# Rounding w_out by column groups in order of use, with seven products in all batches, nine attention slots beside it, and sums over keys in four column tiles

## Chip, cores and metric

One core of one Trainium2 chip. The metric is device time in microseconds (us) of that core, the median of several executions. The kernel before takes 1590.8 us (1589.6 to 1591.5).

## The reference, cut to what matters

```python
# q, k, v: (8, 12, 448, 64) float32; w_in (768, 2048) and w_out (2048, 768): float64
q_n, k_n = rmsnorm(q, g_q), rmsnorm(k, g_k)
scores = scale * q_n @ k_n.T                 # per batch and head
attn = exp(scores - max); attn = attn / (attn.sum(-1) + 1e-9)
x = (attn @ v) -> (3584, 768)                # heads side by side
h = x @ w_in;  g = h - tanh(h)
out = g @ w_out                              # (3584, 768)
```

The weights are float64 and are read as pairs of 32-bit words. The kernel rounds them to float32 itself, with instructions of ScalarE, VectorE and GpSimd.

## The kernel before: the parts that matter

The MLP uses a scheme of seven products in place of eight: seven combinations of weight blocks are made once, put into DRAM, and each batch streams them back through a ring of tiles (`w_f`). Attention goes by *slots*: one slot is two heads of one batch. Between the pieces of a slot, `run(gap)` puts MLP products into TensorE's order of instructions, so that other engines have time for their part.

```python
EARLY = 20                    # pieces of 384 weights per partition rounded in the opening
ring = pool("ring", bufs=6)   # w_f tiles
xp = pool("xp", bufs=9)

def scores(s, half): ...      # 4 score products in 4 "sc" banks, then exponentials on ScalarE
def add(s): ...               # VectorE adds the four key blocks, from the third slot beside the MLP on

def totals(s, dn):            # sum over keys: ones (64 columns), two column tiles
    for i, p in enumerate(parts):
        for h in range(2):
            nc.tensor.matmul(dn[h * D : (h + 1) * D, :S], lhsT=ones[:CP, :D], rhs=p[:, h, :], ...)
    rd = sp.tile([P, S], F32, name="rd")
    nc.vector.reciprocal(rd, dn[:, :S])

def slot(s):
    scores(s + 1, 0)
    load(s + 2, "v")
    run(gap)
    norm(s + 3)
    rd = totals(s, sc_bank())
    divide(s, values(s, sc_bank()), rd)
    run(gap)
    scores(s + 1, 1); add(s + 1)
    run(gap)
    turn(s + 2, sc_bank(), sc_bank()); norm_q(s + 3); load(s + 4, "kq")
    run(gap)

# [cut] project_first: batch 0 takes a plain product with w_out (96 products of 448 columns),
# w_out stays in SBUF while it is rounded; its combinations are made in the second half of it.
```

Six slots stand in the opening, where no weights are ready; three slots stand beside the first part of the MLP and three beside the plain product.

Of the kernel before, what the change touches and what calls it, by code (L numbers as in the profile page):

```python
# [67 lines left out]
def round_weight_a(nc, raw, dst):  # L68

    lo, hi = raw[:, :, 0], raw[:, :, 1]  # L70
    nc.scalar.activation(dst, hi.bitcast(F32), AF.Abs, scale=2.0**-16)
    nc.scalar.mul(lo, lo.bitcast(U32), 2.0**-29)


def round_weight_b(nc, raw, dst):

    bits = dst.bitcast(I32)
    nc.vector.tensor_scalar(out=dst, in0=dst, scalar1=HI_MIN, scalar2=HI_MAX, op0=ALU.max, op1=ALU.min)
    nc.vector.tensor_scalar(  # L79
        out=bits, in0=bits, scalar1=4, scalar2=1, op0=ALU.logical_shift_left, op1=ALU.logical_shift_right  # L80
    )
    nc.vector.scalar_tensor_tensor(  # L82
        out=bits, in0=raw[:, :, 1], scalar=-(2**31), in1=bits, op0=ALU.bitwise_and, op1=ALU.bitwise_or
    )


def round_weight_c(nc, raw, dst):

    bits = dst.bitcast(I32)
    nc.gpsimd.tensor_tensor(out=bits, in0=bits, in1=raw[:, :, 0], op=ALU.add)  # L90


def bounded_path(tc, ctx, q, k, v, moe_w_in, moe_w_out, out, g_col, ident, ones, neg_half):
# [26 lines left out]
    EARLY = 20  # L120
# [4 lines left out]
    STEPS = 7 * (SETS + HC)  # L125
# [6 lines left out]
    ring = pool("ring", bufs=6)  # L132
# [7 lines left out]
    xp = pool("xp", bufs=9)  # L140
    gp = pool("gp", bufs=1)
    wp_stack = ctx.enter_context(ExitStack())
# [9 lines left out]
    def load(s, names):  # L152
# [17 lines left out]
    w_out_sb = [wp.tile([P, DM], F32, name=f"w_out{f}") for f in range(CF)]  # L170
    w_in_dram = {
        (j, p): scratch.tile([P, 2 * HALF], F32, name=f"w_in{j}_{p}") for j in range(SETS) for p in range(1, 8)
    }
    BLOCKS = {1: 0, 2: 1, 4: 2, 7: 3, 5: 4, 6: 5, 3: 6}
    w_out_dram = scratch.tile([P, 7, HC, HF, P], F32, name="w_out")
    w_in_words, w_out_words = weight_words(moe_w_in), weight_words(moe_w_out)
    raws = {}
    stage = gp.tile([P, CF, S], F32, name="gT").bitcast(I32).rearrange("p f s -> p (f s)")
    NSTAGE = CF * S // DM

    def built(j, p):

        return w_out_sb[HF * (j % 2) + p].rearrange("p (f n) -> p f n", f=2)

    def weight_piece(n):

        if n < 2 * CF:
            j, f, blk = n // 8, n % 8 // 4, n % 4
            p, low, i = ((1, 0, 0), (0, 1, 0), (4, 1, 1), (2, 0, 1))[blk]
            return 2 * j + f + low * HF, i, built(j, p)[:, f]  # L190
        i, f = (n - 2 * CF) // CF, n % CF
        if i == 1:
            f = f // 2 + f % 2 * HF
        return f, i, w_out_sb[f][:, i * HALF : (i + 1) * HALF]

    def weight_load(n):

        f, i, _ = weight_piece(n)
        if n < EARLY:
            raw = stage[:, n % NSTAGE * DM : (n % NSTAGE + 1) * DM].rearrange("p (f w) -> p f w", w=2)  # L200
        else:
            raw = wp.tile([P, HALF, 2], I32, name="w_raw", bufs=4)
        if n < 2 * CF:
            rows = w_in_words[i * HALF : (i + 1) * HALF, f * 2 * P : (f + 1) * 2 * P]
            nc.sync.dma_start(
                out=raw.rearrange("p (c f) w -> p c (f w)", c=HC),
                in_=rows.rearrange("(c p) f -> p c f", p=P),
            )
        else:
            nc.sync.dma_start(  # L210
                out=raw.rearrange("p f w -> p (f w)"),
                in_=w_out_words[f * P : (f + 1) * P, 2 * i * HALF : 2 * (i + 1) * HALF],
            )
        raws[n] = raw
# [4 lines left out]
    def place_free(n):  # L219

        if n < EARLY:
            return n - NSTAGE < done[2]
        return n - 4 < max(done[2], EARLY)

    def weight(to):

        while done[1] < min(to, 4 * CF):
            n = done[1]
            round_weight_a(nc, raws[n], weight_piece(n)[2])
            if n:  # L230
                round_weight_b(nc, raws[n - 1], weight_piece(n - 1)[2])
            done[1] = n + 1
            finish_weights(n - 1 if n < EARLY else n)
            while done[0] < min(n + 6, 4 * CF) and place_free(done[0]):
                weight_load(done[0])
                done[0] += 1
            if kept[1] < kept[0] and n >= 8 * kept[0] + 3:
                keep_weights()
        if done[1] == 4 * CF > done[2]:
            round_weight_b(nc, raws[4 * CF - 1], weight_piece(4 * CF - 1)[2])  # L240
            finish_weights(4 * CF)

    def finish_weights(to):
        while done[2] < to:
            round_weight_c(nc, raws.pop(done[2]), weight_piece(done[2])[2])
            done[2] += 1
            if done[2] % 8 == 0 and done[2] <= 2 * CF:
                combine_weights(done[2] // 8 - 1)

    def combine_weights(j):  # L250
        a = [built(j, p) for p in range(8)]
        nc.vector.tensor_tensor(out=a[5], in0=a[0], in1=a[4], op=ALU.add)
        nc.gpsimd.tensor_tensor(out=a[7], in0=a[1], in1=a[0], op=ALU.subtract)
        nc.vector.tensor_tensor(out=a[6], in0=a[5], in1=a[1], op=ALU.subtract)
        nc.vector.tensor_tensor(out=a[3], in0=a[2], in1=a[6], op=ALU.subtract)
        kept[0] = j + 1

    def keep_weights():
        j = kept[1]
        for p in ORDER:  # L260
            nc.sync.dma_start(out=w_in_dram[j, p], in_=built(j, p).rearrange("p f n -> p (f n)"))
        kept[1] = j + 1

    def combine_w_out(f):

        a11, a21 = (w_out_sb[f][:, i * HALF : (i + 1) * HALF] for i in range(2))
        a12, a22 = (w_out_sb[f + HF][:, i * HALF : (i + 1) * HALF] for i in range(2))
        t = [ring.tile([P, 8 * P], F32, name="w_f") for _ in range(2)]
        s3, s1, s2, s4 = (t[i // 2][:, i % 2 * HALF : (i % 2 + 1) * HALF] for i in range(4))
        nc.vector.tensor_tensor(out=s1, in0=a21, in1=a22, op=ALU.add)  # L270
        nc.gpsimd.tensor_tensor(out=s3, in0=a11, in1=a21, op=ALU.subtract)
        nc.vector.tensor_tensor(out=s2, in0=s1, in1=a11, op=ALU.subtract)
        nc.vector.tensor_tensor(out=s4, in0=a12, in1=s2, op=ALU.subtract)
        for n, count, src in ((0, 1, a11), (1, 2, w_out_sb[f + HF]), (3, 2, t[0]), (5, 2, t[1])):
            nc.sync.dma_start(
                out=w_out_dram[:, n : n + count, :, f, :].rearrange("p k c d -> p (k c) d"),
                in_=src[:, : count * HALF].rearrange("p (k d) -> p k d", d=P),
            )
# [4 lines left out]
        for layer, count in ((0, SETS), (1, HC if b else 0))  # L283
# [5 lines left out]
    def ring_load(key, ahead):  # L289

        for n in range(len(ring_tiles), min(ring_steps.index(key) + ahead, len(ring_steps))):
            b, layer, j, p = ring_steps[n]
            t = ring_tiles[ring_steps[n]] = ring.tile([P, 8 * P], F32, name="w_f")
            if layer == 0:
                assert kept[1] > j
                nc.sync.dma_start(out=t[:, : 2 * HALF], in_=w_in_dram[j, p])
            else:
                nc.sync.dma_start(out=t, in_=w_out_dram[:, BLOCKS[p], j].rearrange("p f d -> p (f d)"))


    normed, turned, probs, sums, xT, tt = {}, {}, {}, {}, {}, {}

    def norm(s):

        rr = normed[s] = small.tile([CP, 2, 2 * NCH], F32, name="rr", bufs=3)
        for names in ("q", "k") if s == 0 else ("kq",):
            for name in names:
                rows = loaded[name, s].rearrange("p a b d -> p (a b) d")
                sq = nat.tile([CP, 2 * NCH, D], F32, name="sq", bufs=1)
                nc.gpsimd.tensor_tensor(out=sq, in0=rows, in1=rows, op=ALU.mult)  # L310
# [32 lines left out]

    def sc_bank():
# [694 lines left out]
```

## Time and profile before

| stage of the kernel before | from, to (us) | what limits it |
|---|---|---|
| opening: six slots, first weights | 0 to 117 | VectorE with rounding, by its busy time (the runs do not bear it out, see the end) |
| w_in products of batch 0 | 117 to 264 | nothing is full; TensorE waits for weights that go through DRAM |
| plain product, batch 0 | 264 to 366 | TensorE |
| seven batches, 36 slots | 366 to 1589 | TensorE, granted clock 1.00 |

### The profile page before, as it was taken

What the parts mean: (1) busy time and instruction counts of PE and PEld (TensorE: products, weight loads), DVE (VectorE), ACT (ScalarE), POOL (GpSimd) and SP (SyncE); (2) the same over time, 40 slices, a digit from 0 to 9 for tenths busy, and PEclk for the clock granted to TensorE, in tenths of its full rate; (3) what the DMA queues carried; (4) which work ended last, traced back from release to release, by engine and by line L of the source; (5) the groups of instructions that cost most, each with busy time, mean ns of one, the idle gap of its engine ahead of it and who ended that gap; (6) DMA issues with size and microseconds to landing.
All of it is one profiled execution on the core that took longest, in us unless ns stands there. A gap on an engine that the chain in (4) does not pass through costs nothing.

```text
span 1588.6 us, 19983 instructions
## 1 busy us (share of the span) xinstructions
PE 1494.3 (94%) x7440; PEld 1164.7 (73%) x7440; DVE 788.6 (50%) x1004; ACT 446.4 (28%) x870; POOL 624.4 (39%) x516
## 2 busy tenths in 40 slices
PE   3988768998999999999999999999999999999997
PEld 1336456446878878878877887787877887789997
DVE  6788558865454345434544445434544344522211
ACT  4554234512322223222331232321331232210210
POOL 6655446552452234422453235423444234311410
PEclk9999879999999999999999999999999999999999
DMA  7554575577545554555554564465454664455564
GB/s 193 177 181 165 195 256 166 138 196 229 164 141 161 147 151 144 152 166 148 154 170 123 158 177 131 147 184 139 137 167 133 171 166 137 135 152 162 174 196 105
DMA packets 253983, 257.80 MB, mean 162 GB/s; under 512 B 143413, under 2 KB 198709, under 8 KB 253877
## 3 DMA queue, kind: packets, MB, share of 16 engines
q1 hardware_dynamic: 253552, 256.43, 55.4%
q8 instruction: 61, 1.00, 0.3%
q14 instruction: 46, 0.37, 0.1%
q10 hardware_dynamic: 324, 0.00, 0.0%
HBM read 223.35 MB, written 33.03 MB: 161 GB/s over the span
## 4 chain that ended last, share of the span: by engine, by line
PE 74%; DVE 13%; POOL 3%; DMA 3%; issue 2%; ACT 2%; SPq 2%; ACTq 0%; DVEq 0%; POOLq 0%
PE mb L448 24%; PE ma L448 16%; PE mc L448 15%; PE sc L357 8%; PE sc L383 6%; DVE rd L400 2%; DVE w_out L79 2%; PE sc L395 2%; POOL sq L310 2%; DVE sum L376 2%; DMA w_f<-w_in 1%; PE mb L616 1%; DVE rr L311 1%; ACT p L362 1%; DVE w_out L82 1%
## 5 line engine op out<-in xcount | busy, mean ns | idle before, releaser
L362 ACT ACTIVATE p<-sc,rr 112x448 f32<-112x448 f32 x384 | 212.5, 638 | 224.0 <-PE sc L357 162.0
L448 PE MATMUL mb<-tt,w_f 128*128 128x224 f32 x768 | 166.5, 361 | 17.3 <-DMA w_f<-w_in 16.3
L357 PE MATMUL sc<-qT,kT 64*112 64x448 f32 x768 | 179.5, 574 | 2.2 <-DVE rd L400 1.5
L448 PE MATMUL ma<-xT,w_f 128*128 128x224 f32 x768 | 163.8, 365 | 11.9 <-DMA w_f<-w_in 11.9
L448 PEld LDWEIGHTS mb<-tt,w_f 128*128 128x128 f32 x768 | 142.6, 192 | 42.6 <-issue 22.8
L448 PEld LDWEIGHTS ma<-xT,w_f 128*128 128x128 f32 x768 | 149.7, 197 | 18.7 <-issue 6.2
L315 POOL TENSOR_TENSOR rr<-rr,neg_half 112x16 f32<-112x16 f32 (+1 forms) x49 | 140.7, 2871 | 51.3 <-DVE rr L314 50.3
L400 DVE RECIPROCAL rd<-sc 128x448 f32<-128x448 f32 x42 | 124.0, 2953 | 34.9 <-PE sc L395 34.0
L448 PE MATMUL ma<-gT,w_f 128*128 128x224 f32 x672 | 139.2, 356 | 0.0
L448 PEld LDWEIGHTS ma<-gT,w_f 128*128 128x128 f32 x672 | 125.3, 190 | 15.3 <-issue 15.3
L448 PE MATMUL mb<-tg,w_f 128*128 128x224 f32 x672 | 135.1, 354 | 0.0
L383 PE MATMUL sc<-p,v_nat 112*64 112x448 f32 x672 | 133.4, 539 | 0.0
L448 PEld LDWEIGHTS mb<-tg,w_f 128*128 128x128 f32 x672 | 126.2, 190 | 7.3 <-issue 7.3
L376 DVE TENSOR_TENSOR sum<-sum,p 112x896 f32<-112x896 f32 x80 | 95.8, 1198 | 58.2 <-ACT p L362 52.6
L357 PEld LDWEIGHTS sc<-qT,kT 64*112 64x112 f32 x768 | 65.9, 176 | 79.4 <-issue 62.1
L535 POOL TENSOR_TENSOR u<-u,s 128x448 f32<-128x448 f32 x32 | 36.5, 1141 | 221.0 <-DVE u L534 194.7
L311 DVE TENSOR_REDUCE rr<-sq 112x8 f32<-112x512 f32 x96 | 65.4, 681 | 113.9 <-POOL sq L310 113.9
L310 POOL TENSOR_TENSOR sq<-q_nat 112x512 f32<-112x512 f32 x48 | 50.0, 1041 | 150.5 <-DVE rr L311 103.2
L383 PEld LDWEIGHTS sc<-p,v_nat 112*64 112x64 f32 x672 | 48.3, 137 | 78.0 <-issue 78.0
L448 PE MATMUL mb<-xT,w_f 128*128 128x224 f32 x384 | 87.4, 366 | 17.2 <-DVE s L530 11.4
L504 POOL TENSOR_TENSOR gT<-s,th 128x448 f32<-128x448 f32 x64 | 75.0, 1172 | 62.1 <-ACT th L503 62.1
L448 PEld LDWEIGHTS mb<-xT,w_f 128*128 128x128 f32 x384 | 71.3, 194 | 34.6 <-issue 20.4
(108 smaller groups left out, 2146.0 us busy)
## 6 DMA issues: line engine op xcount, KB each, us to landing
w_f<-w_in SPq DMA_DIRECT2D x224, 384.0 KB, 3.6
w_f<-w_out SPq DMA_DIRECT2D x147, 512.0 KB, 4.3
w_raw<-in_moe_w_out_dram SPq DMA_DIRECT2D x32, 384.0 KB, 3.4
k_nat<-in_k_dram SPq DMA_DIRECT2D x96, 112.0 KB, 3.3
q_nat<-in_q_dram SPq DMA_DIRECT2D x48, 224.0 KB, 3.7
v_nat<-in_v_dram SPq DMA_DIRECT2D x48, 224.0 KB, 4.7
w_in<-w_out SPq DMA_DIRECT2D x28, 384.0 KB, 5.6
out_dram<-th SPq DMA_DIRECT2D x192, 56.0 KB, 2.7
```

The costliest lines, as they stand in the source:

```text
L79: nc.vector.tensor_scalar(out=bits, in0=bits, scalar1=4, scalar2=1, op0=ALU.logical_shift_left, op1=ALU.logical_shift_right)
L310: nc.gpsimd.tensor_tensor(out=sq, in0=rows, in1=rows, op=ALU.mult)
L311: nc.vector.reduce_sum(rr[:, "kq".index(name)], sq, axis=AX.X)
L315: nc.gpsimd.tensor_tensor(out=r, in0=r, in1=neg_half[:, : r.shape[1]], op=ALU.pow)
L357: nc.tensor.matmul(sc[:CP, :S], lhsT=kT[r, c * CP : (c + 1) * CP], rhs=qT[r, :], start=True, stop=True)
L362: nc.scalar.activation(p[:, h, i, :], tiles[h][:CP, :S], AF.Exp, scale=rr[:, 0, 2 * c + h : 2 * c + h + 1])
L376: nc.vector.tensor_tensor(out=t, in0=t, in1=part, op=ALU.add)
L383: nc.tensor.matmul(av[h * D : (h + 1) * D, :S], lhsT=v_nat[:, h, c, :], rhs=p[:, h, c % 2, :], start=(c == 0), stop=(c == NCH - 1),)
L400: nc.vector.reciprocal(rd, dn[:, :S])
L448: nc.tensor.matmul(bank[:, f * HS : (f + 1) * HS], lhsT=w[:, f * depth + c, :], rhs=moving[p](c), start=(first and f == 0 and c == 0), sto ...
L504: eng.tensor_tensor(out=g[:, rows, cols], in0=h, in1=th, op=ALU.subtract)
L535: nc.gpsimd.tensor_tensor(out=u3, in0=u3, in1=s5, op=ALU.add)
```

## The change

The intent: batch 0 gets seven products like the others (8.6 us of TensorE less). For this w_out has to be rounded and combined before its use, so all weights now come as units of seven blocks in the order of use, and nine slots, not six, stand beside the rounding. The sums over keys use 32 columns of ones, so four column tiles work at once and the reciprocal has half the columns. The reciprocals then lie on four partition groups and must be spread over 128 partitions: they go out to DRAM (`rows_out`) and come back broadcast (`rows_in`). So sum and division move apart, and the order of the slot changes. Squares move from GpSimd to ScalarE, into the tile of the normalised q. The diff below is cut to the parts that the argument needs; the opening's slot is reordered in the same way (sum at the end of the slot before, then trip and division), and from the end of the rounding on a fourth place for exponentials is added.

```diff
-    EARLY = 20
+    EARLY = 12          # pieces of 768
+    FAST = 9            # slots beside the rounding
-    ring = pool("ring", bufs=6)
+    ring = pool("ring", bufs=5)
-    xp = pool("xp", bufs=9)
+    xp = pool("xp", bufs=12)
+    def region(u):      # one unit: seven blocks, rounded, combined, then stored
+            regions[u] = wp.tile([P, 7 * HALF], F32, name="w_new", bufs=2)
+    [weight(): store unit u right after piece 2u + 3 was begun]
+            if kept[1] < kept[0] and k >= 2 * kept[1] + 3:
+                keep_weights()
     [norm]
-                sq = nat.tile([CP, 2 * NCH, D], F32, name="sq", bufs=1)
-                nc.gpsimd.tensor_tensor(out=sq, in0=rows, in1=rows, op=ALU.mult)
+                sq = nat.tile([CP, NCH, 2, D], F32, name="n", bufs=1).rearrange(...)
+                nc.scalar.activation(sq, rows, AF.Square)
     [totals]
-                nc.tensor.matmul(dn[h * D : (h + 1) * D, :S], lhsT=ones[:CP, :D], rhs=p[:, h, :], ...)
-        rd = sp.tile([P, S], F32, name="rd")
-        nc.vector.reciprocal(rd, dn[:, :S])
+                for n in range(2):
+                    r = (2 * h + n) * BL
+                    nc.tensor.matmul(dn[r : r + BL, :HS], lhsT=ones[:CP, :BL], rhs=p[:, h, n * HS : (n + 1) * HS], ...)
+        rs = whole[s] = sp.tile([P, HS], F32, name="rs")
+        nc.vector.reciprocal(rs, dn[:, :HS])
+    def rows_out(s):    # rs -> row in DRAM
+    def rows_in(s):
+        nc.sync.dma_start(out=rd,
+            in_=bass.AP(tensor=row.tensor, offset=row.offset, ap=[[S, 2], [0, D], [1, S]]))
     [slot]
         scores(s + 1, 0)
+        totals(s, sc_bank())
         load(s + 2, "v")
-        run(gap)
-        norm(s + 3)
-        rd = totals(s, sc_bank())
-        divide(s, values(s, sc_bank()), rd)
-        run(gap)
-        scores(s + 1, 1); add(s + 1)
-        run(gap)
-        turn(s + 2, ...); norm_q(s + 3); load(s + 4, "kq")
+        run(gap / 2); rows_out(s); run(gap / 2); rows_in(s)
+        turn(s + 2, ...); load(s + 4, "kq"); norm(s + 3)
+        run(gap)
+        if not wide: divide(s, values(s, sc_bank()))      # in the stretch
+        scores(s + 1, 1); add(s + 1)
+        if wide: divide(s, values(s, sc_bank()))          # after it
+        run(gap)
+        norm_q(s + 3)
         run(gap)
```

## The prediction

> **What bounds the kernel now.** I read the page's totals and slices first, then one table by stage (busy time in chosen windows), then the chain of waits, then the instructions of one attention slot. From the page:
>
> ```profile
> PE 1494.3 (94%) x7440; PEld 1164.7 (73%) x7440; DVE 788.6 (50%) x1004; ACT 446.4 (28%) x870; POOL 624.4 (39%) x516
> ...
> PE   3988768998999999999999999999999999999997
> ...
> PEclk9999879999999999999999999999999999999999
> ```
>
> TensorE is full from the tenth slice on, so from there only less TensorE work saves time. The first nine slices are something else. The stage borders are the first product of the MLP (117 us), the first plain product with w_out (264) and the first product of batch 1 (377):
>
> ```profile
> 0.00:117.00 117.00, 82.44 (x372) 33.31 (x373) 90.27 (x123) 56.18 (x111) 70.70 (x54) 0.91 0.64 183
> 117.00:264.00 147.00, 110.83 (x502) 84.17 (x499) 104.01 (x144) 56.36 (x115) 71.86 (x56) 0.87 0.61 199
> 264.00:377.00 113.00, 110.40 (x378) 53.53 (x377) 81.72 (x110) 37.63 (x73) 58.16 (x50) 1.00 0.66 184
> 377.00:1438.00 1061.00, 1048.29 (x5444) 851.69 (x5443) 483.02 (x577) 279.09 (x538) 390.40 (x327) 1.00 0.53 152
> ```
>
> Columns: window, length, PE, PEld, DVE, ACT, POOL, clock, DMA share, GB/s. In the opening (0 to 117) VectorE is busy 90 of 117 us: it and the rounding set the pace. In the second stage VectorE is busy 104 of 147 us and nothing is full. The chain of waits tells why: TensorE stands still for weights that have to go out to DRAM and come back.
>
> ```profile
> 142.92 4.49 DMA w_f<-w_in
> ...
> 161.50 6.49 DMA w_f<-w_in
> ...
> 214.11 4.99 DMA w_f<-w_in
> ```
>
> Then one steady slot on PE, and the groups that matter:
>
> ```profile
> 1014.09 0.97 PE L395 MATMUL sc<-sum,ones 112*64 112x448 f32 x4
> 1014.89 3.18 PE L383 MATMUL sc<-p,v_nat 112*64 112x448 f32 x16
> 1018.00 1.02 PE L448 MATMUL mc<-tg,w_f 128*128 128x224 f32 x4
> ...
> L400 DVE RECIPROCAL rd<-sc 128x448 f32<-128x448 f32 x42 | 124.0, 2953 | 34.9 <-PE sc L395 34.0
> L79 DVE TENSOR_SCALAR w_out<-w_out 128x384 int32<-128x384 int32 x64 | 53.0, 828 | 2.2
> ```
>
> Start to start, the sums over keys take 0.80 us and the values 3.11 us. Each fp32 product shows as two records; 16 records of the MLP take 3.03 us, so a product of 224 columns costs 0.379 us, and a batch (336 products) 127.3 us. After 377 there are 36 slots and 7 batches: (1588.6 - 377 - 5.5 for the last store - 7 x 127.3) / 36 = 8.75 us of TensorE for a slot.
>
> **What the Trainium skill says.** "TensorEngine Tiling (Array Packing)", Overview: with at most 32 stationary columns the array works as four tiles, with 64 as two; under Key Properties, tiles operate independently, and a change of mode drains the array. The trace agrees for two tiles: the values issue 16 records of 448 columns in 3.01 us, 0.188 us each, as long as one 224-column record of the full array. Four tiles no run shows yet. "GPSIMD Engine Reference", Specifications: GpSimd shares its SBUF interfaces with VectorE, with contention from two-input or 2-port instructions. The trace fits: the shift of L79 takes between 359 and 1182 ns for one shape, median 1050, in stages where GpSimd rounds too. "DMA: Bandwidth & Descriptors", Why a DMA increments its semaphore by 16 and not by 1: a transfer is spread over as many engines (up to 16) as divide the slowest dimension of both sides. The new load of the reciprocals reads a pattern whose slowest dimension is 2, so by that page it runs on two engines. Nothing before shows it.
>
> **The change, part by part.**
>
> 1. Plain product with w_out removed. Batch 0 spends 96 products of 448 columns, 192 records at 0.376 us, 72.2 us. With seven products it is 63.6. Saved 8.6 us of TensorE. The combinations of w_out are made anyway, now earlier.
>
> 2. Attention beside rounding. Before, by 377 us the kernel has 12 slots and one batch of MLP. After, the rounding ends at product 37 of batch 0 (28 + 9 of 21), with 6 + 9 slots done: 63.6 + 27.3 = 91 us of MLP and 15 slots. The stretch of nine slots needs of TensorE 91 + 9 x (8.75 - 0.80 + 1.5 for unsummed keys) = 176 us. VectorE in it: 15360 elements per partition to round (4 pieces of 768, 24 of 512) at 1.94 us per 384 (mean of L78 0.457, L79 0.828, L82 0.651) = 78; combinations, 8 of 384 at 0.6 and 48 of 256 at about 0.45 = 26; nine slots of two reductions 1.37, scale 0.18, reciprocal 1.5, q 0.9, division 0.97 = 44; MLP results 4 x 4.35 + 3 = 20. Together 168 us. So TensorE and VectorE are matched. The best sample of how well they share is 264 to 377: VectorE 81.7 of 113 (72%), TensorE about 100 us of real work (72 plus three slots), 88%. I take 84% of TensorE: 176 / 0.84 = 210 us. The weights are kept in smaller lots (one unit at a time, 1.4 MB, not seven transfers at once), with five or more products between keeping and use, so the waits of 4 to 6 us should shrink but not vanish.
>
> 3. The opening. The pieces grow from 20 of 384 to 12 of 768, 20% more, about 39 to 42 us of VectorE with fewer fixed costs; combinations rise from 7.8 us to about 13.6; six reciprocals fall from 2.95 to 1.5 us (half the columns), -8.7; squares leave GpSimd for ScalarE, which has 61 us free there. Sum -1 to -4 us on VectorE: 117 becomes 114.
>
> 4. Sums in four tiles. In a steady slot 0.75 us at the record rate becomes 0.375 if four tiles run at once. But they now follow four score products directly and need a fifth bank of four, which the first exponential frees about 1.7 us after the scores start, just when TensorE arrives. I count 0.25 of the 0.375, for 33 slots: 8 us. The reciprocal gets shorter and the division moves two gaps later, so the wait of TensorE for rd that shows once in each batch (1.4 us of six idle spots) goes: 8 us; the wait at 377 for the first w_f (4.3) too. I count 10 of these 12.
>
> After the stretch there remain 8 x 127.3 - 91 = 927 of MLP, 33 x 8.5 = 281 of attention, 5.5 of store, less 10: 1204.
>
> Sum: 114 + 210 + 1204 = 1528 of span, and 2 more for the time against the span (1590.8 against 1588.6): **1530 us**.
>
> **Rivals.**
>
> A: the way through DRAM. Row sums go out, come back broadcast, and SyncE waits for each in order; ring loads stand behind. On two engines the load is 64 rows of 1792 bytes each, an estimate of 5 us from packets of 1 KB at 46 ns uncontended in this trace, beside about 2 for the issue. The chain reciprocal, out, in is some 11 us; in the nine slots only two gaps of 2.5 us and the transposes lie between sum and division, so VectorE, in order, would wait up to 3 us a slot while being nearly full. For: VectorE is near its limit there. Against: its own queue of rounding lies between the two. It makes the stretch 235 to 245, the total 1555 to 1565. In steady slots the gaps are near 5.7 us and hide it; if not, ring loads (three ahead, not four) come late and each slot loses 1 us: 1563.
>
> B: DMA becomes the bound in the stretch. It moves about 51 MB there besides the broadcasts (raw 13, kept 15, ring 16.5, q, k, v 6): 245 GB/s at 210 us, where windows of 20 us before reach 282 at a share of 0.82. Bursts will cost something, and the two engines of the broadcast more. It makes about the same, 1550 to 1570.
>
> C: better than thought. If smoother keeping lets TensorE run at 93% as in the later stages, the stretch is 190 us; with all of the sums' gain the total is 1503.
>
> D: four tiles gain nothing, because twice as many weight loads and records are issued. Then +8 steady and +14 in the stretch: 1550.
>
> **Range and chances.** The stretch carries the spread: 190 to 245 around 210. The opening adds 6 either way, the steady part from -5 to +20. I set 1500 to 1570. Faster by over 2% means below 1559; only A or B at nearly full size, or two of A, B and D together, prevent it: 80% faster, 16% same, 4% slower. Slower needs the steady slots to wait for ring loads, against the four products of time that each load still has.
>
> **What would show it.** Right: the first MLP product near 114, the last rounding near 324 instead of 322 with three more slots done, PE busy over 80% between; a steady sum over keys near 0.4 us start to start; reciprocals at 1.5 us. Wrong: VectorE waiting long for the landing of rd (A); PE waiting for w_f beyond 400 us (A); DMA share above 0.85 through the stretch (B); totals at 0.75 us (D); an opening over 122 us. A table load before each square would be a cost that I have not counted: before, one load served the whole run.

## More of the kernel before

Where a stage is full of TensorE work, only less TensorE work helps. In the other stages the question is which wait ends last. The lines that show this are in the prediction, with one border read wrongly there: the prediction begins the seven batches at 377 us. TensorE's timeline of the kernel before has their first product at 366.27:

```profile
366.27 2.54 PE L448 MATMUL ma<-xT,w_f 128*128 128x224 f32 x12
```

At 377 a wait of 4.6 us for weights begins.

## The result, and the profile after

The changed kernel takes **1691.3 us** (1689.4 to 1695.7, four runs), 6.4% slower: ratio 1.0636, 95% interval 1.0615 to 1.0658. A ratio here is the mean time of one kernel's fast runs over that of the other's of the same rounds, so not quite the ratio of the medians quoted. 1530 was predicted.

From the page of the kernel after: totals, two rows of the 40 slices, and the reciprocals:

```profile
PE 1510.1 (89%) x8040; PEld 1206.2 (71%) x8040; DVE 689.9 (41%) x975; ACT 495.5 (29%) x922; POOL 521.8 (31%) x395
...
PE   5653687787699999999999999889999999999998
...
PEclk9776888888799999999999999999999999999999
...
L395 DVE RECIPROCAL rs<-sc 128x224 f32<-128x224 f32 x42 | 65.4, 1556 | 129.0 <-PE sc L390 128.8
```

TensorE is now not full before the 12th slice (of 42 us). VectorE (690 against 789 us) and GpSimd (522 against 624) work less than before, ScalarE (496 against 446, with the squares) and TensorE (1510 against 1494) somewhat more. The kernel is 100 us slower, so most of the time went into waiting. The table by stage for the kernel after (window, length, PE, PEld, DVE, ACT, POOL, clock, DMA share, GB/s):

```profile
0.00:171.00 171.00, 88.88 (x504) 36.62 (x504) 99.15 (x129) 71.30 (x120) 50.25 (x28) 0.78 0.55 160
171.00:451.00 280.00, 212.99 (x1090) 141.37 (x1090) 138.80 (x223) 103.78 (x188) 105.47 (x74) 0.85 0.60 187
451.00:1544.00 1093.00, 1065.96 (x5700) 888.71 (x5700) 422.42 (x571) 303.57 (x580) 332.74 (x262) 0.99 0.56 160
```

The first MLP product starts at 171.4 us, the last record of product 37 (where the rounding was to be done) starts at 450.7, the span ends at 1693.8. Against the prediction: opening 171 for 114 (+57), stretch of nine slots 279 for 210 (+69), the rest 1243 for 1204 (+39). (The 117 of the prediction for the kernel before was the first scores after the opening; its first product starts at 120.4, so 120.4 is the figure to compare with 171.4.) In opening and stretch no engine is over 76% busy, and DMA is at a share of 0.55 to 0.60. The granted clock fell too (0.78 and 0.85, for 0.91 and 0.87 before), so TensorE's busy time also contains slower products.

The waits of the kernel after, up to 640 us (engine, line, what ended the wait: us in total, times, longest), show two that have no counterpart in the kernel before:

```profile
DVE xT L417 <- DMA rd<-row: 79.9, 12, 12.8
...
ACT w_new L71 <- DMA w_out<-w_new: 67.0, 7, 14.9
```

and ScalarE's own list of waits adds a third of the same kind:

```profile
ACT w_new L71 <- DMA w_in<-w_new: 27.6, 4, 12.9
```

VectorE waits for the broadcast reciprocals, and ScalarE waits, before its first write into a place for fresh weights, for the store of the unit that lay there. In the trace, what stands behind in the order of these engines waits with them. The timeline of the kernel after in the opening shows one wait of each kind, down to TensorE:

```profile
58.26 0.57 SPq L408 DMA_DIRECT2D rd<-row  x1
67.26 0.95 DVE L417 TENSOR_TENSOR xT<-ma,rd 128x448 f32<-128x448 f32 x1 [7.71 <-DMA rd<-row]
68.26 4.92 PE L376 MATMUL ma<-p,v_nat 112*64 112x448 f32 x16 [2.39 <-DVE xT L417]
...
103.98 0.59 SPq L264 DMA_DIRECT2D w_in<-w_new  x1
...
110.39 0.89 ACT L71 ACTIVATE w_new<-gT 128x768 f32<-128x768 f32 x1 [12.94 <-DMA w_in<-w_new]
...
112.61 3.85 PE L350 MATMUL sc<-qT,kT 64*112 64x448 f32 x8 [7.00 <-ACT p L355]
```

The broadcast is issued at 58.26, and the division starts at 67.26: VectorE idled for 7.7 us. At 103.98 a unit of weights is stored; ScalarE starts the next unit in its place at 110.39 after idling 12.9 us. The exponentials that stand behind it come late, and TensorE's next scores wait 7.0 us for a bank that those exponentials free.

The DMA view of the kernel after from 58 to 68 us (40 slices of 0.25 us: busy tenths of 16 engines, then GB/s) shows how the broadcast moves:

```profile
DMA  0435989999986357589999987753212121111111
GB/s 0 90 106 152 270 307 311 315 373 369 352 299 204 118 106 129 188 235 316 336 354 343 241 219 220 247 169 88 82 59 75 71 76 67 59 45 49 41 49 41
```

The trace has 128 packets of 1792 bytes (224 KB) for each broadcast. Those of this one run from 61.2 to 66.7 us beside packets of raw weights; from 65 us on the sixteen engines are at a share of one or two tenths and at most 82 GB/s. The times of the 128 packets add up to 10.4 us in 5.5 us, so about two are in flight at once; over all broadcasts it is 1.7 to 2.1. That fits the two engines of the prediction's rival A.

### The profile page after: what moved, and what is told of

It is laid out like the page before. It is cut to its first block, busy times and chain, and to the rows that moved or that the text cites. A ratio compares the mean times of both kernels' runs of the same rounds, so it can differ in the third digit from the quotient of the medians.

```text
span 1693.8 us, 21146 instructions
## 1 busy us (share of the span) xinstructions
PE 1510.1 (89%) x8040; PEld 1206.2 (71%) x8040; DVE 689.9 (41%) x975; ACT 495.5 (29%) x922; POOL 521.8 (31%) x395
## 5 line engine op out<-in xcount | busy, mean ns | idle before, releaser
L350 PE MATMUL sc<-qT,kT 64*112 64x448 f32 x768 | 198.0, 597 | 48.3 <-ACT p L355 28.9
L470 PE MATMUL mb<-tg,w_f 128*128 128x224 f32 x768 | 159.5, 358 | 0.1
L470 PE MATMUL ma<-gT,w_f 128*128 128x224 f32 x768 | 156.7, 354 | 2.0 <-POOL gT L526 1.8
L470 PEld LDWEIGHTS mb<-tg,w_f 128*128 128x128 f32 x768 | 145.8, 193 | 8.6 <-issue 7.0
L470 PEld LDWEIGHTS ma<-gT,w_f 128*128 128x128 f32 x768 | 143.9, 190 | 7.3 <-issue 4.6
L376 PE MATMUL sc<-p,v_nat 112*64 112x448 f32 x672 | 140.6, 562 | 9.2 <-ACT p L355 9.1
L299 DVE TENSOR_REDUCE rr<-n 112x8 f32<-112x512 f32 x96 | 65.8, 685 | 172.6 <-ACT n L298 172.4
L395 DVE RECIPROCAL rs<-sc 128x224 f32<-128x224 f32 x42 | 65.4, 1556 | 129.0 <-PE sc L390 128.8
L369 DVE TENSOR_TENSOR sum<-sum,p 112x896 f32<-112x896 f32 x66 | 79.9, 1211 | 68.0 <-ACT p L355 63.6
L470 PE MATMUL mc<-tt,w_f 128*128 128x224 f32 x384 | 80.5, 357 | 4.7 <-DMA w_f<-w_in 4.7
```

The costliest lines, as they stand in the source:

```text
L299: nc.vector.reduce_sum(rr[:, "kq".index(name)], sq, axis=AX.X)
L350: nc.tensor.matmul(sc[:CP, :S], lhsT=kT[r, c * CP : (c + 1) * CP], rhs=qT[r, :], start=True, stop=True)
L369: nc.vector.tensor_tensor(out=t, in0=t, in1=part, op=ALU.add)
L376: nc.tensor.matmul(av[h * D : (h + 1) * D, :S], lhsT=v_nat[:, h, c, :], rhs=p[:, h, c % 2, :], start=(c == 0), stop=(c == NCH - 1),)
L395: nc.vector.reciprocal(rs, dn[:, :HS])
L470: nc.tensor.matmul(bank[:, f * HS : (f + 1) * HS], lhsT=w[:, f * depth + c, :], rhs=moving[p](c), start=(first and f == 0 and c == 0), sto ...
```

## The experiments

Theory: the two waits (trip through DRAM, places for fresh weights) hide each other and hold opening and stretch; the order of the slot costs time in the rest. Rivals: DMA is the bound; the four tiles gain nothing; the rounding is bound by one engine. In the two kernels made from the kernel before (b1, b2) the stages differ, so only the first product and the slot are given. The runs of the kernel before beside these had medians of 1589.7 to 1591.7.

All correct except e14. "First product" is the start of the first MLP product, "stretch" goes from there to the start of the last record of product 37, "rest" to the end of the span, all in the profiled run, which can lie a few us off the median. "Slot" is TensorE time for one slot by the prediction's own account: from the start of the last record of product 37 to that of the last MLP record, less 0.18943 us for each of the 4896 MLP records between (127.3 us for 672), divided by the slots that are left (33; 36 in e13). For before, b1 and b2 it is the time of the seven batches from their first product on, for 36 slots.

| run | us | ratio to before, 95% | first product | stretch | rest | slot |
|---|---|---|---|---|---|---|
| before | 1590.8 | 1 | 120.4 | - | - | 8.97 |
| after | 1691.3 | 1.0615 to 1.0658 | 171.4 | 279.3 | 1243.1 | 9.33 |
| e1_slots | 1684.3 | 1.0580 to 1.0615 | 172.3 | 274.2 | 1235.6 | 9.09 |
| e2_rd16 | 1655.5 | 1.0399 to 1.0434 | 154.7 | 265.1 | 1232.3 | 8.99 |
| e3_no_trip | 1675.3 | 1.0506 to 1.0557 | 152.8 | 279.5 | 1242.3 | 9.29 |
| e4_slots_no_trip | 1628.5 | 1.0229 to 1.0263 | 146.1 | 239.7 | 1239.8 | 9.20 |
| e5_slots_rd16 | 1633.4 | 1.0261 to 1.0295 | 155.5 | 245.3 | 1229.0 | 8.89 |
| e6_sq_gpsimd | 1648.3 | 1.0351 to 1.0393 | 153.5 | 248.2 | 1245.1 | 9.37 |
| e7_sq_tile | 1628.9 | 1.0225 to 1.0259 | 146.3 | 240.3 | 1241.9 | 9.28 |
| b1_sums | 1638.2 | 1.0282 to 1.0317 | 135.0 | - | - | 9.85 |
| e9_first_loads | 1620.0 | 1.0169 to 1.0203 | 130.7 | 247.2 | 1239.9 | 9.21 |
| e10_order | 1617.1 | 1.0143 to 1.0177 | 146.5 | 253.2 | 1220.5 | 8.62 |
| e11_all | 1598.3 | 1.0025 to 1.0059 | 121.6 | 255.7 | 1220.7 | 8.64 |
| b2_order | 1639.4 | 1.0292 to 1.0327 | 125.7 | - | - | 9.58 |
| e12_steady4 | 1594.1 | 1.0000 to 1.0034 | 121.4 | 255.1 | 1216.3 | 8.49 |
| e13_fast6 | 1605.1 | 1.0077 to 1.0113 | 121.3 | 234.0 | 1247.1 | 8.66 |
| e14_no_comb (wrong) | 1581.9 | 0.9928 to 0.9961 | 118.0 | 240.8 | 1219.9 | 8.61 |
| e15_all4 | 1607.5 | 1.0084 to 1.0113 | 121.1 | 268.2 | 1217.0 | 8.52 |
| e16_s4_gpsimd | 1599.4 | 1.0040 to 1.0072 | 121.4 | 260.7 | 1216.3 | 8.50 |
| e17_best | 1592.4 | 0.9993 to 1.0020 | 121.8 | 254.1 | 1217.1 | 8.54 |

### Two waits that hide each other: e1 to e5

**e1_slots**: four places for fresh weights while w_in is rounded and three for w_out, for two. The added ones lie in the still unused tile of the token factors (tg) and in the space that a unit of w_out leaves.

```diff
-            regions[u] = wp.tile([P, 7 * HALF], F32, name="w_new", bufs=2)
+    w_new = wp.tile([P, 14 * HALF], F32, name="w_new")
+    first = first_tg.rearrange("p a f s -> p (a f s)")     # the tile of tg, unused so far
+        if u < HF:
+            src, at = ((w_new, 0), (w_new, 1), (first, 0), (first, 1), (w_new, 0), (w_new, 1), (first, 1), (w_new, 0))[u]
+        else:
+            src, at = w_new, 2 - (u - HF) % 3
```

> Only the room for freshly rounded weights is changed: four places instead of two in the opening (two of them in a tile that is idle there) and three instead of two while w_out is rounded, in the same memory; everything else is the changed kernel (1691 us). Theory 1 (two places are too few: ScalarE waits 94.6 us in 11 waits for the stores of the place it is about to write, and exponentials stand behind it): ScalarE's waits for those stores fall under 20 us and the time falls by 45 to 75 us, to 1615 to 1645. Theory 2 (the way of the reciprocals through DRAM is what costs): under 20 us gained, 1670 to 1690.

Measured: only 7 us less, 1684.3. The waits went as theory 1 said: in e1 no wait for those stores is left in ScalarE's list. The time did not: VectorE's waits for rd grew from 79.9 to 88.3 us.

**e2_rd16**: the broadcast as one load for each head, whose slowest dimension is 64.

```diff
-        nc.sync.dma_start(out=rd, in_=bass.AP(..., ap=[[S, 2], [0, D], [1, S]]))
+        for h in range(2):
+            nc.sync.dma_start(out=rd[h * D : (h + 1) * D, :],
+                in_=bass.AP(tensor=row.tensor, offset=row.offset + h * S, ap=[[0, D], [1, S]]))
```

> The changed kernel with the broadcast load of the reciprocals split by head, so that the slowest dimension of each load is 64 and not 2. Its 128 packets of 1792 bytes now take 4.8 to 6.3 us from first to last at two in flight. If a load is spread over as many engines as divide its slowest dimension, the packets should pass in about 1 us, and VectorE's 79.9 us of waits for the broadcast should fall to about half. Theory 2: 15 to 35 us faster (1655 to 1675). Theory 1: under 15 us.

Measured: 36 us less. The timeline of e2_rd16 shows the same broadcast as above:

```profile
57.09 1.14 SPq L409 DMA_DIRECT2D rd<-row  x2
62.57 0.99 DVE L418 TENSOR_TENSOR xT<-ma,rd 128x448 f32<-128x448 f32 x1 [4.16 <-DMA rd<-row]
```

From issue to division it takes 5.5 us in place of 9.0, and VectorE's idle time before it falls from 7.7 to 4.2. All of VectorE's waits for rd fall from 79.9 to 33.8 us, while ScalarE's waits for the stores grow from 94.6 to 108.4.

**e3_no_trip**: the old sums in two tiles with the reciprocal of 448 columns, and no way through DRAM, in the order of the kernel after (`rows_out` and `rows_in` empty, `totals` as before).

> The changed kernel with the sums over keys as before: two column tiles of 64, reciprocal of 448 columns at once, no way through DRAM. Theory 2: VectorE's waits for the broadcast vanish (79.9 us, 67 of them before 451 us), the opening falls from 171 to about 135 us and the time to 1625 to 1650, although a steady sum costs 0.25 us more (8 us in all) and each reciprocal 1.4 us of VectorE. Theory 1: 1670 to 1690, for ScalarE still waits for the stores.

**e4_slots_no_trip**: e1 and e3 together.

> Both: more places for the weights and no way through DRAM. If the two causes are separate and add up: 1560 to 1600, and the opening back to 115 to 125 us. If one hides the other: no better than the better of the two alone by more than 15 us. If it is still above 1620, a third cause (the order of the queue of SyncE, or GpSimd against VectorE) holds.

**e5_slots_rd16**: e1 and e2 together.

> More places for the weights (as e1) and the broadcast on all engines (as e2). Alone they gave 7 and 36 us. If the two-engine broadcast was what held VectorE while the places held ScalarE, so that each hid behind the other, the sum is larger than 43: 1615 to 1635, near e4 (1628) and with shorter steady sums. If they only add, 1648.

Measured: without the trip 16 us less, with places as well another 46.8 (e4, 1628.5). Places alone gave 7, on top of e3 they gave 47. So each wait hid the other, and the traces of e1 and e2 show it: whichever was taken away, the other grew (by 8 and by 14 us). Alone, neither shows its size: e1 by itself spoke for theory 2, e3 (1675.3) for theory 1. By the expectation of e4 a time above 1620 means a third cause; the later runs find two, the slot's order and the queue of SyncE. In e4 ScalarE's list of waits in the first 450 us has only this left of the stores:

```profile
ACT w_new L71 <- DMA w_in<-w_new: 3.8, 1, 3.8
```

With places and sixteen engines (e5) the time is 1633.4, 5 us above e4: the trip costs more in opening and stretch (15 us: 155.5 + 245.3 against 146.1 + 239.7) than the four-tile sums give back in the rest (11 us).

### Squares, a miss: e6 and e7

**e6_sq_gpsimd** puts the squares back on GpSimd with their own tile, on top of e4. **e7_sq_tile** leaves them on ScalarE and only gives them their own tile.

```diff
-                sq = nat.tile([CP, NCH, 2, D], F32, name="n", bufs=1).rearrange(...)
+                sq = nat.tile([CP, 2 * NCH, D], F32, name="sq", bufs=1)
-                nc.scalar.activation(sq, rows, AF.Square)
+                nc.gpsimd.tensor_tensor(out=sq, in0=rows, in1=rows, op=ALU.mult)     # e6 alone
```

> e4 with the squares back on GpSimd and in a tile of their own, as in the kernel before. Theory 3: on ScalarE the squares stand in one queue with the exponentials, and each second square waits for the reduction of the first on VectorE (ScalarE waits 35.7 us for that in the opening of e4); the opening falls from 146 to about 120 us and the time to 1590 to 1605. Rival: GpSimd is then slower with the rounding and VectorE slower beside it, and nothing is gained (1620 to 1635).

> e4 with the squares left on ScalarE but in a tile of their own, not in the one of the normalised q. If it is the shared tile that couples them, this gains as much as e6 (to 1590 to 1610). If it is the engine, under 8 us (1620 to 1630), because square, reduction and next square still take turns in one tile.

Measured: e6 is 20 us slower than e4, more than even its rival had said, and e7 is no different. Squares on ScalarE are a good part of the change, and the shared tile costs nothing.

### The order of the slot: b1, b2, e10

**b1_sums** puts the four-tile sums, the trip and the new order into the kernel before. **b2_order** puts in the order alone, with the old sums and without a trip. Both take, in all slots, the order that the kernel after has in its opening and stretch (values before the second scores); after the stretch the kernel after has the values behind those scores (`wide`), and the transposes are left in their old place.

```diff
 # b2_order, slot(), on the kernel before (b1_sums: with rows_out and rows_in in the gaps)
         scores(s + 1, 0)
+        totals(s, sc_bank())
         load(s + 2, "v")
         run(gap / 2); run(gap / 2)
         norm(s + 3)
-        rd = totals(s, sc_bank())
-        divide(s, values(s, sc_bank()), rd)
         run(gap)
+        divide(s, values(s, sc_bank()))
         scores(s + 1, 1); add(s + 1)
```

> The kernel before (1590) with one part of the change alone: sums over keys in four column tiles, the way through DRAM on two engines, and sum and division moved in the slot as in the change. By my prediction's terms a steady sum is 0.25 us shorter: 36 slots make 9 us, and the idle waits for rd (8 us) go, so 1570 to 1580. By theory 2 the opening alone loses 20 to 35 us to the broadcast: 1595 to 1625 in all.

> The kernel before with the moved sum and division alone (order of b1), but the sums as before and no way through DRAM. b1 lost 48 us: 15 in the opening, 22 to the end of the first batch, and about 1 us in each later slot. If the way through DRAM costs that: 1585 to 1600. If the order does (values straight ahead of scores, a fifth bank of four wanted): 1615 to 1635.

Measured: b2_order costs 49 us by itself (1.031), a little more than the order's theory had said, and b1_sums, with the sums and the trip besides, is the same within a microsecond or two. So in the kernel before the order accounts for the whole loss. That the trip is free there is not shown: b1's first product comes at 135.0 against 125.7 in b2, and what made up for it was not separated. The timeline of TensorE in b2_order shows one place where the order costs:

```profile
1021.65 3.23 PE L383 MATMUL sc<-p,v_nat 112*64 112x448 f32 x16
1024.80 2.35 PE L357 MATMUL sc<-qT,kT 64*112 64x448 f32 x8
1027.08 1.78 PE L454 MATMUL mb<-tt,w_f 128*128 128x224 f32 x8
```

The scores take 2.35 us where they take 1.76 elsewhere. Values and the four score products need five of the four "sc" banks, and the values hold theirs until VectorE has divided. To see where it goes, I summed, over slots 24 to 47 of each trace, the time from each TensorE record's start to the next one's start by its kind (16 records of scores, 16 of values, 4 or 8 of sums in a slot; none is missing). In us for one slot, the mean and, where it differs, the median in brackets:

| kind | before | b2_order | after | e7_sq_tile | e10_order | e12_steady4 |
|---|---|---|---|---|---|---|
| scores | 3.43 (3.38) | 4.21 (3.85) | 3.84 (3.45) | 3.87 (3.45) | 3.38 | 3.38 |
| sums over keys | 0.80 | 0.90 | 0.52 | 0.90 | 0.80 | 0.52 |
| values | 3.11 | 3.16 | 3.32 (3.16) | 3.38 (3.16) | 3.11 | 3.16 |

The four-tile sums gain 0.28 us in the kernel after, which is about what was counted (0.25). The order takes back 0.41 at the scores and 0.21 at the values on average, but not in every slot: by the medians it is 0.07 and 0.05. In the kernel after, the rest stands in three places, at 1058.5, 1128.2 and 1452.5 us, where the values stand straight behind scores and wait 2 to 5 us for a bank; the values after the first two of these waits also take 4.9 and 5.4 us for 3.16. At the first of them the exponential that frees the bank stands, in ScalarE's order, behind a tanh that waits 6.1 us for VectorE, which in turn waits for GpSimd. With MLP products between scores and values (e10) no such wait is left. In b2_order it is different: there every second half of the scores takes about 2.07 for 1.69 us, and 4.2 once in a batch.

**e10_order**: e7 with the order of the kernel before.

> e4 with squares in a tile of their own (e7, 1629 us, the same as e4) and the order inside a slot as in the kernel before: sum, values and division together after the first gap, transposes in the third. After the stretch e4 pays 9.19 us of TensorE a slot against 8.75 before, and shows waits of values for exponentials right behind the scores. If the order is what costs, the part after product 37 gets 12 to 18 us shorter and the time 1611 to 1618; if the waits come from elsewhere, 1625 to 1635.

Measured: 11.8 us less than e7; the slot falls from 9.28 to 8.62 and the rest from 1241.9 to 1220.5, while the stretch grows by 13. There the order of the kernel after was the better one.

### The start of the MLP: e9 and e11

**e9_first_loads**: the loads of the first four weight tiles of the ring are issued before the last slot of the opening, not when the first product comes.

```diff
     def first_slot(s):
+        if s == NP - 1:
+            ring_load((0, 0, 0, 1), 4)
```

> e4 with the first four ring loads issued a slot earlier, ahead of the store of a later unit that stands before them in the queue of SyncE. In e4 the first MLP product waits 15.3 us for them (19.4 in the changed kernel, 2.5 before). If that wait is the queue's order: 1612 to 1618, the wait under 4 us. If other work (rounding of the next pieces, the exponentials) would have held TensorE anyway: 1624 to 1630.

The timelines of e4_slots_no_trip

```profile
119.88 0.58 SPq L269 DMA_DIRECT2D w_in<-tg  x1
...
137.66 0.57 SPq L269 DMA_DIRECT2D w_in<-w_new  x1
...
138.98 4.21 SPq L288 DMA_DIRECT2D w_f<-w_in  x5
...
146.15 4.29 PE L463 MATMUL ma<-xT,w_f 128*128 128x224 f32 x12 [14.80 <-DMA w_f<-w_in]
```

and of e9_first_loads

```profile
119.49 0.57 SPq L269 DMA_DIRECT2D w_in<-tg  x1
120.11 3.84 SPq L288 DMA_DIRECT2D w_f<-w_in  x4
...
130.69 2.54 PE L463 MATMUL ma<-xT,w_f 128*128 128x224 f32 x12
```

show why. In e4 the ring loads stand in SyncE's queue behind the store of a later unit, issued at 137.66 because VectorE had not combined it earlier. The first product doesn't need that unit, yet it waits 14.8 us. In e9 the loads go right after the store before it, and the first product starts at 130.7, 15.5 us earlier. Of these the total keeps 8.5: the stretch gets 7.5 longer.

**e11_all**: e7 with e9's loads, the order of e10 and EARLY = 10, so that 20 pieces of 384, as before, are rounded in the opening.

> e7 with both of the above and only 10 pieces rounded in the opening, as much as before (not 12). If all add: opening 125 to 132 us (146 in e4), total 1580 to 1598, about the kernel before. If it stays above 1605, the stretch itself (more rounding work on VectorE and larger pieces on GpSimd) holds the rest.

Measured: 1598.3 us, 18.8 less than e10. The first product starts at 121.6, close to the 120.4 of the kernel before.

### What holds the stretch, and a better version: e12 to e17

**e12_steady4**: e11 with four-tile sums and their trip on sixteen engines in the 33 slots after the stretch only, and with MLP products between every two users of the "sc" banks. `rs` lies in the tile of the added keys, so no memory is needed for it.

```diff
+    def steady(s, gap):          # after scores(s + 1, 0); slots after the stretch
+        load(s + 2, "v"); run(gap / 2)
+        totals4(s, sc_bank()); run(gap / 2)
+        out4(s); norm(s + 3); run(gap / 2)
+        in4(s); run(gap)
+        divide(s, values(s, sc_bank())); run(gap / 2)
+        scores(s + 1, 1); add(s + 1); run(gap / 2)
+        turn(s + 2, ...); norm_q(s + 3); load(s + 4, "kq"); run(gap / 2)
```

> e11_all (1598) with the four-tile sums and their way through DRAM (on 16 engines) put back only in the 33 slots after the stretch of nine, with a gap of MLP between the sums and the scores, and the values two and a half half-gaps later. Theory, that the sums gain 0.25 us a slot once the order keeps TensorE from waiting: minus 8 us, 1590. Rival, that the trip costs something there whatever the order: 1598 or more. Nothing before the 361st microsecond should move.

Measured: 1594.1, 4.2 us less than e11, half of the 8 expected, and 8.49 us for a slot: the 8.5 of the prediction. The sums gain 0.28 us a slot as before; values (3.16 for 3.11) and MLP products beside them give part of it back. TensorE's timeline of e12_steady4:

```profile
1001.07 3.23 PE L382 MATMUL sc<-p,v_nat 112*64 112x448 f32 x16
1004.23 1.40 PE L493 MATMUL ma<-xT,w_f 128*128 128x224 f32 x6
...
1020.72 0.59 PE L407 MATMUL sc<-sum,ones 112*32 112x224 f32 x8
1021.23 1.02 PE L493 MATMUL mb<-xT,w_f 128*128 128x224 f32 x4
```

The sum takes 0.51 us start to start (before: 0.80), and nothing waits around it. So the sums pay and the trip hides (VectorE's list has no wait for rd<-row), where the gaps are wide and the order leaves TensorE alone. The list of TensorE's waits after the stretch of e12 has none for w_f either, so the smaller ring, which was not tested by itself, shows no cost there.

**e13_fast6**: e11 with FAST = 6.

> e11_all with six attention slots beside the rounding in place of nine. What a slot costs inside the stretch: if the stretch of 240 us is held by rounding, GpSimd and DMA whatever stands beside, it shortens by under 15 us, and the three slots cost 26 us later: 1608 to 1612. If slots cost their TensorE and VectorE time there, it shortens by 33 to 40 and the total is 1586 to 1594.

**e14_no_comb**: e11 without the four combinations of each unit, their places zeroed once.

> e11_all without the four combinations of each unit of weights (their places are zeroed once at the start, so the result is wrong on purpose). They are 34 us of VectorE, some 25 of it in the stretch. If VectorE with the combinations in its order holds the stretch at 240 us: minus 20 to 25 there, minus 5 in the opening, total 1570 to 1576. If GpSimd's last addition or DMA holds it: minus 5 to 10, total 1588 to 1594.

**e15_all4**: e12 with the four-tile sums, the trip and the wide order in the nine slots of the stretch too.

> e12_steady4 (1594) with the same four-tile sums, their trip on 16 engines and the same order of the slot in the nine slots beside the rounding too (the opening keeps the old sums). Removed there: 9 x 1.4 us of reciprocals on VectorE and 9 x 1.5 us on TensorE. Theory, that VectorE and TensorE share the hold on the stretch, so that about two thirds of what VectorE is spared shows (as in e14, 16 of 25): minus 8 to 15, 1579 to 1586, under before (1590). Rival A of the prediction, that the gaps of 2.5 us there can't hide the trip: VectorE waits 2 to 4 us a slot for rd, 1594 to 1620.

**e16_s4_gpsimd**: e15 with the last combination of each unit on GpSimd. **e17_best**: e12 with the same edit.

```diff
-                nc.vector.tensor_tensor(out=s4, in0=a12, in1=s2, op=ALU.subtract)
+                nc.gpsimd.tensor_tensor(out=s4, in0=a12, in1=s2, op=ALU.subtract)
```

> e15_all4 with the last of the four combinations of each unit on GpSimd. If VectorE's time is what counts (6 us of it in the stretch): minus 3 to 5 against e15_all4. If the engines' sharing of SBUF or the chain to the store takes it back: the same or slower.

> e12_steady4 (1594, old sums in the stretch, four-tile sums after it) with the last combination of each unit on GpSimd, which took 8 us off e15_all4. If VectorE's time is what counts in the stretch without the trip too: 1585 to 1589, just under before (1591). If e16's gain came from VectorE's waits for rd, which e12 has not: 1592 to 1595.

The tables by stage of the stretch, columns as above, for e11_all:

```profile
121.60:377.30 255.70, 213.89 (x976) 136.92 (x976) 180.16 (x261) 109.75 (x194) 114.51 (x79) 0.89 0.75 226
```

for e13_fast6:

```profile
121.30:355.30 234.00, 178.89 (x808) 126.47 (x808) 165.08 (x240) 89.34 (x158) 106.78 (x76) 0.86 0.74 230
```

for e14_no_comb:

```profile
118.00:358.80 240.80, 208.29 (x977) 135.78 (x976) 155.99 (x193) 110.62 (x195) 116.97 (x80) 0.91 0.80 237
```

and for e15_all4:

```profile
121.10:389.30 268.20, 215.50 (x1120) 141.47 (x1120) 159.35 (x258) 109.85 (x194) 113.78 (x79) 0.86 0.72 224
```

Three slots fewer take 35 us off TensorE and 15 off VectorE, and the stretch falls by 21.7. The combinations take 24 us off VectorE alone, and it falls by 14.9. In both runs the stretch fell between the two theories of the expectation, so neither theory is right by itself. It seems that no single engine holds the stretch: what one is spared shows by about six tenths (21.7 of 35, 14.9 of 24), though in e13 two engines are spared at once. DMA isn't the bound of e11: without the combinations it moved more, 237 GB/s at a share of 0.80. (The granted clock was 0.91 in e14 against 0.89; what part of the gain that is can't be separated.)

e15 missed in the other direction. VectorE is spared 21 us against e11, and the stretch is 13.1 us longer than in e12. Its waits in the stretch name the trip again:

```profile
DVE xT L444 <- DMA rd<-row: 16.3, 4, 9.6
```

So on sixteen engines, with places enough and a new order, the trip still costs there, as rival A said: the gaps are too short to hide it. e15 changes the order in the stretch as well, so the 13 us are for both. The combination moved to GpSimd takes 8.1 us off e15 (e16, 1599.4), but off e12 only 1.7, with the two ratios' intervals overlapping (e17, 1592.4). That speaks for the rival of e17's expectation: e16's gain was mostly in VectorE's waits behind the trip.

e17 equals the kernel before: ratio 1.0006, interval 0.9993 to 1.0020. No correct version that I ran beats the kernel before; the repaired change gives back everything that it lost and no more. Its rounding ends late: in e12 the last addition of a rounding ends at 362 us, in the kernel before at 323, and 324 was predicted.

## Why the prediction was wrong

- **The opening: "Sum -1 to -4 us on VectorE: 117 becomes 114."** This step failed, with the largest error for its size: 171.4. It added up VectorE's busy time and took the order of work as given. VectorE was busy 99 us of the 171, not some 87, and the other 72 are waits. It looked for the trip's wait in the nine slots only (rival A), and the six slots of the opening have no gaps of MLP at all: sixteen engines alone took 17 us off there, no trip 19. The 20% more of early rounding was counted as busy time alone, and the queue at the first product not at all; e11 shows 121.6 with both mended. The premise that VectorE "and the rounding set the pace" is not borne out either: up to the first product VectorE is busy 80.0 us in e11 and 93.6 in the kernel before, and the first product is no earlier.
- **"The weights are kept in smaller lots ... the waits of 4 to 6 us should shrink."** Failed. I looked at the reader's side, the ring loads, and not at the writer's: with two places, ScalarE soon comes to write into the place whose store has just been issued. That made 94.6 us of ScalarE's waits and 47 us of time (e3 to e4).
- **"I take 84% of TensorE: 176 / 0.84 = 210 us."** Failed. The sample for it, 264 to 377 of the kernel before, is a stage that TensorE fills, and its end was misread: the about 98 us of TensorE work that were counted are done by 366, which makes 96%, not 88. Such a stage could not show what a stretch loses that waits for fresh weights. In the repaired e12 the stretch is 255 us for about 190 us of clean TensorE work (176 plus nine times 1.5 for the old sums): 74%. e13 and e14 show that work of both engines counts in part. What sets this share in detail stays open; the larger pieces and the smaller number of places for raw weights were not tested by themselves.
- **Four tiles.** "I count 0.25 of the 0.375" was right: 0.28 measured in the kernel after. Rival D, no gain, is refuted. But the order that came with it took back 0.41 + 0.21 us a slot on average, most of it in a few long waits. I had seen that the sums need a fifth bank, and took this for a loss in the gain of the sums; that values straight behind scores also wait for a bank, and long where the exponential is late, was not seen.
- **The rest, "8.75 us of TensorE for a slot" and "I count 10 of these 12".** The 8.75 was 0.2 to 0.3 too low, because the seven batches were taken to begin at 377: the same sum from 366.3 on gives 9.05, and 8.97 with the 8.5 us that really follow the last product (5.5 were counted). The waits that were to vanish did: TensorE's 8.1 us in six waits became 1.4 in the kernel after and 1.0 in e11. (The trace puts them down to VectorE's sums `s`, not to rd.) But in the kernel after new ones came: 9.1 us for exponentials, 6.6 for a division, 5.2 for w_f. The slot cost 9.33, not 8.5. With the mended order it is 8.49, and the rest of e12 is 1216.3. So 1204 was 12 too low even for the best order: some 10 of these are the border and 3 the time after the last product.
- **Rival A** had the mechanism: two engines, VectorE waiting in order. Its size was off: 5 us of transfer and up to 3 us of wait in a slot of the stretch, where the trace has 9.0 from issue to division, waits of up to 12.8, and the opening besides. The mend (e2) is worth 36 us. **Rival B** had a share above 0.85 in the stretch as its sign; it was 0.60.
- **Right**: the reciprocal at 1.5 us (1.556), the squares on ScalarE (e6), the first idle slices as the place where most is decided (126 of the 165 us). The table load before each square, named as a cost not counted, did not come: either trace has one table load.

From 1691.3 down to the best version, 1592.4, the causes in the order in which I took them away are: places and trip together 62.8 us (1691.3 to e4, 1628.5), the slot's order 11.8 (e7 to e10), queue order at the first product and less rounding in the opening 18.8 (e10 to e11), four-tile sums put back where they pay 4.2 (e11 to e12), one combination on GpSimd 1.7. Another order would give other shares, since they hide each other. The profiled span of e17, 1593.0, is still 65 us above the predicted span of 1528: the stretch (44), the rest (13) and the opening (8).

## What to carry to other kernels

When a change puts waits of several kinds on engines that work in order, taking one away can show little (here 7 and 16 us of 63): take them away in pairs before calling one harmless. For each buffer of a store, ask what is written next into its place and how long after the issue, not only who reads what was stored. Before moving a step to another place in a loop, count the banks of its neighbours: an instruction that comes straight after a user of all banks waits for the first of them to be freed, and this can cost more than the step itself saves (0.78 us a slot at the scores of b2_order, where the shorter sums save 0.28). And before calling a mean over slots a cost of each slot, look at the median: here it was a few long waits.

## What the Trainium skill lacked or had wrong

- "DMA: Bandwidth & Descriptors", Why a DMA increments its semaphore by 16 and not by 1: its rule for the number of engines fits a broadcast load from DRAM (slowest dimension 2: the 128 packets take 4.8 to 6.3 us with about two in flight; split by head, 2.5 us in the one looked at, and 36 us less in the whole). The page tells how to split one contiguous dimension; it does not say that a broadcast of this kind is better issued as several loads.
- "TensorEngine Tiling (Array Packing)", Theoretical Speedup: up to twice from 64 to 32 columns. Measured: 0.80 to 0.52 us for a sum over keys that stands alone between MLP products (1.5 times), for 4 records of 448 columns against 8 of 224. The page has no figure for so short a group.
- "SBUF — State Buffer", SBUF: two separate sides: the port pair shared by VectorE and GpSimd is an exclusive lock, and the loser fully blocks. The trace of the kernel after agrees, and shows that VectorE can lose to two GpSimd instructions in a row, which the page doesn't say. Its timeline:

```profile
97.84 3.85 POOL L90 TENSOR_TENSOR w_new<-w_new,gT 128x768 int32<-128x768 int32 x2
98.13 3.97 DVE L251 TENSOR_TENSOR w_new<-w_new 128x384 f32<-128x384 f32 x1
...
102.21 0.56 DVE L252 TENSOR_TENSOR w_new<-w_new 128x384 f32<-128x384 f32 x1
```

  A combination of 384 elements takes 0.56 us alone. Beside two GpSimd additions one is shown as 3.97 us, until 0.41 us after the second of them ended.
- No page that I read has a figure for what TensorE loses when users of PSUM banks follow each other directly. Here (medians of e7 against e10) it is 0.04 us at four scores, 0.1 at the sums and 0.05 at the values of a slot, and 2 to 5 us where the exponential that frees the bank is late.
